# One step for both head groups: the products with k and v of batches 2 to 7 in a fused attention and expert kernel

## The chip, the cores and the metric

The kernel runs on one core of a Trainium2 chip. A core has TensorE (PE in the profile, with its weight loads as PEld), VectorE (DVE), ScalarE (ACT), GpSimd (POOL) and SyncE (SP); in this kernel SP does nothing but issue DMAs, and POOL issues some as well. The metric is device time in microseconds (us). One execution was profiled; the others were only timed.

## The reference

For 8 batches and 8 heads, with sequence 576, head width 64 and 32 memory slots, the attention is

```python
a = softmax(phi, over the sequence)          # (b, h, 576, 32)
k_m = einsum('bhsm,bhsd->bhmd', a, k)        # 32 x 64 per head
v_m = einsum('bhsm,bhsd->bhmd', a, v)
attn = softmax(q @ k_m.T / 8)                # (b, h, 576, 32)
x = attn @ v_m                               # 4608 rows of 512
```

and its result feeds four dense experts, weighted per row: `out += p[:, e] * (relu(x @ w1[e]) @ w2[e])`, with 512 inputs, 1024 hidden and 512 outputs. The change concerns the two einsums: the contraction over the 576 sequence places that gives k_m and v_m.

## The kernel before, in words

The kernel never forms x. It multiplies v_m with w1 (helper `vw_mm`, L433) and applies the attention weights to that product (`first`, L548 to L550; six matmuls in a step, three for each of two weight halves because operands are split into a high and a low part). `second` (L581 to L583) multiplies the hidden values with w2.

**Steps.** The first part of the program, up to about 400 us, is a list of 128 steps. Each step `s` emits, in this order: `accumulate()`, then `run_plan(s)`, then `first(s + 2)` and `second(s)`. Every engine runs its own instructions in the order in which they were emitted. `run_plan(s)` emits whatever the table `plan` holds for step `s`: the attention of the next batches, the splits of w2, stores and loads. The rest of the program, from step 128, works by another scheme and is not touched.

**Attention of batch b** (`attention`, L649 onward) hangs on a number `turn` from the table `ATT`: 30, 46, 62, 77, 92 and 107 for batches 2 to 7. At `turn` and after, exp(phi) is transposed; at `turn + 6` the products for the first four heads (group 0) run, at `turn + 9` those of the other four (group 1); each is read out of its accumulator by ScalarE one step later (`kv_out`, L304); at `turn + 11` both are transposed (`kv_fold`, L312), and at `turn + 12` copied (`kv_pick`).

**One group's product** is two calls of `kv_mm` (`c2` = 0 and 1), each with eight matmuls of a 32-column weight (L292) that read one staged tile of k and v, 128 x 1024 numbers or 512 KB; the second call adds four matmuls with the tail of the sequence (L298). A batch so needs four staged tiles, two for each group.

**Staged tiles.** All tiles that are streamed in (k and v, q, the raw w2) pass through one sequence, `order`, in the order in which the steps take them, and through four buffers of 512 KB. Taking tile i (`take`) emits the load of tile i + 3 on SP's queue. SP runs its queue strictly in order and does not keep to the steps: a load starts when all issues ahead of it have gone out and its buffer has been read by everyone who reads it. Which of the four buffers a load gets is fixed when the program is built, and with it whom it waits for. A w2 tile is read in two steps, by ScalarE (L153) and then by POOL (L154), once for each half.

In the same 128 steps SP's queue carries w1 (L158), phi (L238), the tail (L242), w2 once more for sums of its columns (`sv`, L191), the exchange of v_m (`vs`, L475), outputs (L606) and, near the end, w2 halves written earlier (`w<-kw`, L752).

Of the kernel before, what the change touches and what calls it, by code (L numbers as in the profile page):

```python
# [51 lines left out]
    7: (99, 107, (2 * PAIR + 112, 2 * PAIR + 116, 2 * PAIR + 123), (2 * PAIR + 120, 2 * PAIR + 125, 2 * PAIR + 131)),  # L52
}

SCORES_0 = ((2, 0), (4, 1))
SCORES_1 = ((0, 8), (2, 9), (4, 13))
VW_1 = (11, 15)
# [24 lines left out]
def body(ctx: ExitStack, tc: tile.TileContext, qm, qt, kv, kvt, phi, prob, w1, w1d, w2, out):  # L82
# [8 lines left out]
    def bank(tag, *shape):  # L91
        n = idle[tag].popleft()
        out = banks[:, n, :]
        m = 1
        for d in shape:
            m *= d
        names = "abcd"[:len(shape)]
        out = out[:, :m].rearrange(
            f"p ({' '.join(names)}) -> p {' '.join(names)}", **dict(zip(names, shape))
        )  # L100
        lent[id(out)] = tag, n, out
        return out

    def give(ps):
        tag, n, _ = lent.pop(id(ps))
        idle[tag].append(n)
# [128 lines left out]
    def load_phi(b):  # L235
        ph = att.tile([P, 2, S], F32, name="ph", tag="ph")
        for g in range(2):
            nc.sync.dma_start(ph[:, g], phi[b, g])  # L238
        st["ph", b] = ph

    def load_tail(b):
        nc.sync.dma_start(kvt_t[64:], kvt[b])  # L242

    def phi_max(b, g):
        nm = att.tile([P, 1], F32, name="nm", tag="nm", bufs=2)
        nc.vector.reduce_max(nm, st["ph", b][:, g], AX.X)
        nc.vector.tensor_scalar_mul(nm, nm, -1.0)
        st["nm", b, g] = nm

    def phi_exp(b, g):  # L250
        ph = st["ph", b][:, g]
        zs = att.tile([P, 1], F32, name="zs", tag="zs", bufs=4)
        nc.scalar.activation(ph, ph, AF.Exp, bias=st["nm", b, g], accum_out=zs)
        st["zs", b, g] = zs

    def phi_norm(b, g):
        zs = st["zs", b, g]
        nc.vector.tensor_scalar_add(zs, zs, 1e-9)
        nc.vector.reciprocal(zs, zs)

    def phi_turn(b, g):
        if g == 0:
            st["a", b] = att.tile([P, 2, NC, P], F32, name="a", tag="a")
        ph = st["ph", b]
        tp = bank("pm", 4, P)
        for c in range(4):
            nc.tensor.transpose(tp[:, c], ph[:, g, c * P:c * P + P], ident)
        st["tpa", b, g] = tp

    def phi_turn_out(b, g, copy=nc.scalar.copy):  # L270
        copy(st["a", b][:, g, :4], st["tpa", b, g])
        give(st["tpa", b, g])

    def phi_turn_tail(b):

        tp = bank("pm", 2, P)
        for g in range(2):
            nc.tensor.transpose(tp[:, g], st["ph", b][:, g, S - P:], ident)
        st["tpb", b] = tp

    def phi_turn_tail_out(b, copy=nc.scalar.copy):
        copy(st["a", b][:, :, 4], st["tpb", b])
        give(st["tpb", b])

    def kv_mm(b, g, c2, raw):
        if c2 == 0:
            st["x", b, g] = bank("pm", P)
        x, a = st["x", b, g], st["a", b]
        for i in range(2):
            for h in range(4):  # L290
                m = slice(M * h, M * h + M)
                nc.tensor.matmul(  # L292
                    x[m], a[:, g, 2 * c2 + i, m], raw[:, i, h], start=c2 + i == 0, stop=False,
                    skip_group_check=True,
                )
        for h in range(4 if c2 else 0):
            m = slice(M * h, M * h + M)
            nc.tensor.matmul(  # L298
                x[m], a[:, g, 4, m], kvt_t[:, 4 * g + h], start=False, stop=True, skip_group_check=True
            )  # L300

    def kv_out(b, g):
        xs = att.tile([P, 2 * P], F32, name="xs", tag="xs", bufs=3)[:, :P]
        nc.scalar.activation(xs, st["x", b, g], AF.Copy, scale=st["zs", b, g])  # L304
        give(st["x", b, g])
        st["xs", b, g] = xs

    def kv_fold(b, gs=range(2)):
        for g in gs:
            if g == gs[0]:  # L310
                st["kvp", b, g] = bank("pm", len(gs), P)
            nc.tensor.transpose(st["kvp", b, gs[0]][:, g - gs[0]], st["xs", b, g], ident)  # L312

    def kv_pick(b, gs=range(2), copy=nc.scalar.copy):
        src = st["kvp", b, gs[0]]
        n = 2 * len(gs)
        copy(
            kvm[b % 6][:, 2 * gs[0]:2 * gs[0] + n].rearrange("p a j m -> p (a j m)"),
            src.rearrange("p g m -> p (g m)"),
        )  # L320
        give(src)
# [14 lines left out]
    def scores_mm(b, t0, q, hps=range(NP)):  # L336

        nt, n = tiles(t0)
        if hps[0] == 0:
            st["sT", b, t0] = [bank("pm", 256) for _ in range(2)]  # L340
        sT = st["sT", b, t0]
        for hp in hps:
            for i in range(2):
                half, m = slice(64 * i, 64 * i + 64), slice(M * hp, M * hp + M)
                nc.tensor.matmul(
                    sT[i][m, :nt * n], kvm[b % 6][half, hp, i], q[half, hp, :nt * n],
                    start=True, stop=True,
                )
# [49 lines left out]
    def q_key(b, t0):  # L398
        return ("qm", b, t0 // 2) if t0 < 4 else ("qt", b)
# [60 lines left out]
    def v_split(b):  # L460

        vh = att.tile([P, 2, NP, M], F32R, name="vh", tag="xs", bufs=3)
        for j in range(2):
            r = v_half(j)
            split(vh[r], kvm[b % 6][r, :, j], nc.gpsimd)
        st["vh", b] = vh

    def write_v(b):

        if b == 4:  # L470
            st["vs"] = att.tile([P, 2, NP, P], F32R, name="vs", tag="vs")
        c = slice(M * (b - 4), M * (b - 4) + M)
        for j in range(2):
            for i in range(2):
                nc.sync.dma_start(  # L475
                    st["vs"][64 * i:64 * i + 64, j, :, c].bitcast(F32),
                    st["vh", b][v_half(j), i].bitcast(F32),
                )
# [139 lines left out]
    def at(s, unit):  # L618
        plan[s].append(unit if isinstance(unit, tuple) else (None, unit))

    def scores_quick(b, t0, n):

        at(n, (q_key(b, t0), lambda q: (scores_mm(b, t0, q), scores_copy(b, t0))))
        at(n + 1, lambda: (scores_turn(b, t0), scores_max(b, t0)))
        at(n + 2, lambda: (scores_exp(b, t0), soft_sum(b, t0)))
        at(n + 3, lambda: soft_scale(b, t0, nc.vector))
        at(n + 4, lambda: (transposes(b, t0), transposes_out(b, t0)))
# [5 lines left out]

    for t0, n in SCORES_0:
        scores_quick(0, t0, n)
# [19 lines left out]
    def attention(b, s, turn, scores, turns):  # L655

        at(s, lambda: load_phi(b))
        at(turn, lambda: load_tail(b))
        for g in range(2):
            at(s + 3, lambda g=g: phi_max(b, g))  # L660
            at(s + 4, lambda g=g: phi_exp(b, g))
            at(s + 5, lambda g=g: phi_norm(b, g))
            at(turn + g, lambda g=g: phi_turn(b, g))
            at(turn + 1 + g, lambda g=g: phi_turn_out(b, g))
        at(turn + 2, lambda: phi_turn_tail(b))
        at(turn + 3, lambda: phi_turn_tail_out(b))
        for g in range(2):
            for c2 in range(2):
                at(turn + 6 + 3 * g, (("kv", b, g, c2), lambda raw, g=g, c2=c2: kv_mm(b, g, c2, raw)))
            at(turn + 7 + 3 * g, lambda g=g: kv_out(b, g))  # L670
        at(turn + 11, lambda: kv_fold(b))
        at(turn + 12, lambda: kv_pick(b))
        if b >= 4:
            at(turn + 15, lambda: v_split(b))
            at(turn + 17, lambda: write_v(b))
        for t0, n in zip((0, 2, 4), scores):
            at(n, (q_key(b, t0), lambda q, t0=t0: scores_mm(b, t0, q)))
            plan[n + 1].insert(0, (None, lambda t0=t0: scores_copy(b, t0)))
            at(n + 2, lambda t0=t0: scores_turn(b, t0))
            at(n + 3, lambda t0=t0: scores_max(b, t0))  # L680
            at(n + 4, lambda t0=t0: scores_exp(b, t0))
            at(n + 5, lambda t0=t0: soft_sum(b, t0))
            at(n + 6, lambda t0=t0: soft_scale(b, t0, nc.gpsimd))
        for t0, n in zip((0, 2, 4), turns):
            at(n, lambda t0=t0: transposes(b, t0))
            at(n + 1, lambda t0=t0: transposes_out(b, t0))
# [27 lines left out]
    for b in range(2, B):  # L714
        attention(b, *ATT[b])
# [288 lines left out]
    with tc.manual_schedule():  # L1004
        raw = {}
# [9 lines left out]
        raw = {key: take(later) for later, key in enumerate(early)}  # L1015
# [128 lines left out]
```

## Time and profile before

| | us |
|---|---|
| median of 3 timed runs | 1333.23 (1332.06 to 1333.5) |
| profiled execution, own time | 1333.66 |
| its span | 1331.9 |
| PE busy | 1313.2 (99%) |
| DVE busy | 813.6 (61%) |
| POOL busy | 587.2 (44%) |
| ACT busy | 535.8 (40%) |

The clock granted to TensorE is shown as a share of full speed; over the span its mean was 0.999. "Idle before" in a row of the timeline is time in which the engine had nothing running, followed by what ended it. A DMA row with "q" behind the engine is the issue of a transfer, not the transfer; its time to landing is told in the view of the DMAs. Line numbers are those of the kernel before; in the changed kernel the lines behind the new table are one higher.

### The profile page before, as it was taken

The numbers are of one execution on the slowest core, as the hardware profiler recorded it, in microseconds if no ns is written. First come the engines' busy times: TensorE is split into PE (matmuls) and PEld (weight loads), VectorE is DVE, ScalarE is ACT, GpSimd is POOL, SyncE is SP. The second block draws the span as 40 slices with busy tenths as digits, with TensorE's granted clock in tenths as the row PEclk, the third lists the DMA queues.
The fourth block names the chain that finished last, engine by engine and source line by source line (L and its number), as shares of the span: only waits on it lengthen the run. The fifth ranks groups of instructions, "written<-read, shape, count | busy, mean of one in ns | idle before, by whom it ended". The sixth has DMA issues, their size and how long they took to land.

```text
span 1331.9 us, 27463 instructions
## 1 busy us (share of the span) xinstructions
PE 1313.2 (99%) x10232; PEld 1192.4 (90%) x10232; DVE 813.6 (61%) x1882; ACT 535.8 (40%) x1303; POOL 587.2 (44%) x666
## 2 busy tenths in 40 slices
PE   8999999999999999999999999999999999999998
PEld 6777878877889888889999999999999999999998
DVE  3544545444336676767666766767677766666665
ACT  3424435435223443333445445554434333333332
POOL 1104336314104553333576677776744433433342
PEclk9999999999999999999999999999999999999999
DMA  8445966956634663234479999999976865656551
GB/s 295 136 180 185 340 221 217 356 185 231 218 131 186 254 252 118 94 143 159 174 261 347 339 342 321 313 330 321 305 218 190 250 189 169 178 163 187 165 171 72
DMA packets 93014, 296.53 MB, mean 223 GB/s; under 512 B 16977, under 2 KB 18129, under 8 KB 92881
## 3 DMA queue, kind: packets, MB, share of 16 engines
q1 hardware_dynamic: 74448, 227.66, 52.5%
q0 software_dynamic: 17280, 62.92, 12.1%
q10 hardware_dynamic: 1152, 4.19, 0.8%
q8 instruction: 81, 1.33, 0.4%
q14 instruction: 53, 0.43, 0.1%
HBM read 217.65 MB, written 76.55 MB: 221 GB/s over the span
## 4 chain that ended last, share of the span: by engine, by line
PE 88%; DMA 4%; DVE 4%; issue 2%; POOL 1%; ACT 1%; SPq 0%; DVEq 0%; POOLq 0%; ACTq 0%
PE banks L891 35%; PE banks L805 7%; PE banks L807 7%; PE banks L806 7%; PE banks L582 4%; PE banks L581 4%; PE banks L583 4%; PE banks L548 2%; PE banks L494 2%; PE banks L433 2%; DMA v<-sv 2%; PE banks L550 2%; PE banks L549 2%; PE banks L929 2%; PE banks L930 2%; PE banks L931 2%
## 5 line engine op out<-in xcount | busy, mean ns | idle before, releaser
L909 DVE SCALAR_TENSOR_TENSOR acc<-banks,pt,acc 128x256 f32<-128x256 f32 x624 | 298.7, 480 | 172.6 <-PE banks L891 168.4
L891 PE MATMUL banks<-w,half 128*128 128x256 f32 x2016 | 300.5, 282 | 1.9 <-DVE acc L909 1.9
L891 PEld LDWEIGHTS banks<-w,half 128*128 128x128 f32 x2016 | 272.4, 189 | 13.4 <-DVE acc L909 4.2
L807 PE MATMUL banks<-AT,vw 128*128 128x256 f32 (+1 forms) x768 | 227.7, 296 | 0.0
L806 PE MATMUL banks<-AT,vw 128*128 128x256 f32 (+1 forms) x768 | 227.4, 296 | 0.0
L805 PE MATMUL banks<-AT,vw 128*128 128x256 f32 (+1 forms) x768 | 227.2, 296 | 0.0
L872 POOL TENSOR_TENSOR half<-g,half 128x512 fp32r<-128x512 f32 x96 | 124.6, 1298 | 158.3 <-ACT half L871 112.6
L154 POOL TENSOR_TENSOR w<-stage,w 128x512 fp32r<-128x512 f32 x96 | 126.0, 1316 | 110.5 <-ACT w L153 108.3
L882 POOL TENSOR_TENSOR n<-xs,n 128x256 fp32r<-128x256 f32 x96 | 70.9, 739 | 174.6 <-ACT n L881 88.1
L805 PEld LDWEIGHTS banks<-AT,vw 128*128 128x128 f32 x768 | 145.4, 189 | 0.9 <-DVE hm L820 0.2
L806 PEld LDWEIGHTS banks<-AT,vw 128*128 128x128 f32 x768 | 144.8, 189 | 0.1
L807 PEld LDWEIGHTS banks<-AT,vw 128*128 128x128 f32 x768 | 144.5, 188 | 0.0
L857 ACT ACTIVATE half<-banks 128x512 fp32r<-128x512 f32 x96 | 57.4, 598 | 207.1 <-DVE g L863 165.2
L562 DVE SCALAR_TENSOR_TENSOR h<-banks,h 128x256 fp32r<-128x256 f32 x128 | 53.8, 421 | 119.0 <-ACT h L560 78.2
L207 POOL TENSOR_TENSOR sv<-sv 128x512 fp32r<-128x512 f32 x32 | 41.2, 1291 | 138.1 <-DVE sv L201 94.9
L582 PE MATMUL banks<-w,h 128*128 128x512 f32 x256 | 100.9, 394 | 0.0
L581 PE MATMUL banks<-w,h 128*128 128x512 f32 x256 | 100.7, 393 | 0.0
L583 PE MATMUL banks<-w,h 128*128 128x512 f32 x256 | 100.7, 393 | 0.0
L560 ACT ACTIVATE h<-banks 128x256 fp32r<-128x256 f32 x128 | 49.0, 384 | 110.5 <-PE banks L550 105.7
L881 ACT CAST n<-xs 128x256 fp32r<-128x256 f32 x96 | 38.6, 402 | 134.2 <-DVE xs L879 134.2
L863 DVE SCALAR_TENSOR_TENSOR g<-banks,g 128x256 f32<-128x256 f32 x192 | 72.3, 418 | 26.6 <-PE banks L807 23.6
L819 ACT ACTIVATE hm<-banks 128x128 fp32r<-128x128 f32 x96 | 26.7, 278 | 152.3 <-DVE xs L879 119.4
(133 smaller groups left out, 2718.4 us busy)
## 6 DMA issues: line engine op xcount, KB each, us to landing
w<-kw SPq DMA_DIRECT2D x91, 512.0 KB, 5.8
w<-v SPq DMA_DIRECT2D x82, 512.0 KB, 5.4
vwd<-vst POOLq DMA_DIRECT2D x64, 512.0 KB, 6.4
vw<-vwd SPq DMA_DIRECT2D x256, 128.0 KB, 5.8
stage<-in_kv SPq DMA_DIRECT2D x32, 512.0 KB, 6.0
w<-in_w SPq DMA_DIRECT2D x32, 512.0 KB, 7.1
v<-sv POOLq DMA_DIRECT2D x32, 512.0 KB, 6.2
stage<-in_w1d SPq DMA_DIRECT2D x32, 512.0 KB, 5.8
```

Source lines behind the costliest of these rows:

```text
L154: eng.tensor_sub(dst[:, 1, :], raw, dst[:, 0, :].bitcast(F32))
L581: nc.tensor.matmul(po[t], x[:, 0, :], w[:, 0, :], start=j == 0, stop=False)
L582: nc.tensor.matmul(po[t], x[:, 0, :], w[:, 1, :], start=False, stop=False)
L583: nc.tensor.matmul(po[t], x[:, 1, :], w[:, 0, :], start=False, stop=j == NJ - 1)
L805: nc.tensor.matmul(ps, w[:, 0, f], at_t[:, g, 0, c], start=g == 0, stop=False)
L806: nc.tensor.matmul(ps, w[:, 0, f], at_t[:, g, 1, c], start=False, stop=False)
L807: nc.tensor.matmul(ps, w[:, 1, f], at_t[:, g, 0, c], start=False, stop=g == 1)
L863: VE.scalar_tensor_tensor(d[:, i], src, 0.0, g[:, 1 + i], ALU.max, ALU.subtract)
L872: GP.tensor_sub(D[:, 1], d, D[:, 0].bitcast(F32))
L882: GP.tensor_sub(N4[:, 1], n, N4[:, 0].bitcast(F32))
L891: nc.tensor.matmul(ps, a[:, l, jj], w[:, r, c], start=start and jj + i == 0, stop=jj == 1 and i == 2, skip_group_check=True,)
L909: VE.scalar_tensor_tensor(a, src, p, a, ALU.mult, ALU.add)
```

## The change

A new table, `KV_AT`, names for each of batches 2 to 7 one step at which all four products of the batch are emitted, group 0 and then group 1; both results are read out in the step behind it.

```diff
+KV_AT = {2: 36, 3: 52, 4: 68, 5: 86, 6: 101, 7: 113}
 ...
         for g in range(2):
             for c2 in range(2):
-                at(turn + 6 + 3 * g, (("kv", b, g, c2), lambda raw, g=g, c2=c2: kv_mm(b, g, c2, raw)))
-            at(turn + 7 + 3 * g, lambda g=g: kv_out(b, g))
+                at(KV_AT[b], (("kv", b, g, c2), lambda raw, g=g, c2=c2: kv_mm(b, g, c2, raw)))
+            at(KV_AT[b] + 1, lambda g=g: kv_out(b, g))
         at(turn + 11, lambda: kv_fold(b))
         at(turn + 12, lambda: kv_pick(b))
```

For batches 2, 3, 4 and 7 the step is `turn + 6`: group 1 moves three steps forward. For batches 5 and 6 it is `turn + 9`: group 0 moves three steps back. No instruction is added or removed. Steps of the products, before and now:

| batch | group 0 before | group 1 before | both now |
|---|---|---|---|
| 2 | 36 | 39 | 36 |
| 3 | 52 | 55 | 52 |
| 4 | 68 | 71 | 68 |
| 5 | 83 | 86 | 86 |
| 6 | 98 | 101 | 101 |
| 7 | 113 | 116 | 113 |

On PE, batch 2 before, around steps 36 and 39. `stage_1271`, `stage_1324`, `stage_1371` and `stage_1400` are the batch's four staged tiles in their order; the matmuls that read AT are `first`.

```order
L583 MATMUL banks_72<-w2_1303,h_1336 128x512
L292 MATMUL banks_72<-stage_1271,a_1248 32x128 x8
L292 MATMUL banks_72<-stage_1324,a_1248 32x128 x8
L298 MATMUL banks_72<-tail_84,a_1248 32x128 x4
L548 MATMUL banks_72<-AT_279,vw_1092 128x256
```

```order
L583 MATMUL banks_72<-w2_1373,h_1432 128x512
L292 MATMUL banks_72<-stage_1371,a_1248 32x128 x8
L292 MATMUL banks_72<-stage_1400,a_1248 32x128 x8
L298 MATMUL banks_72<-tail_84,a_1248 32x128 x4
L548 MATMUL banks_72<-AT_279,vw_1006 128x320
```

The same place in the changed kernel:

```order
L584 MATMUL banks_72<-w2_1303,h_1336 128x512
L293 MATMUL banks_72<-stage_1271,a_1248 32x128 x8
L293 MATMUL banks_72<-stage_1324,a_1248 32x128 x8
L299 MATMUL banks_72<-tail_84,a_1248 32x128 x4
L293 MATMUL banks_72<-stage_1371,a_1248 32x128 x8
L293 MATMUL banks_72<-stage_1400,a_1248 32x128 x8
L299 MATMUL banks_72<-tail_84,a_1248 32x128 x4
L549 MATMUL banks_72<-AT_279,vw_1092 128x256
```

The third and fourth tile are now read directly behind the first two, with nothing of `first` or `second` between.

On SP's queue, batch 6 before. The batch's four tiles are `stage_3155`, `stage_3214`, `stage_3299` and `stage_3309`; `stage_3266` is the last raw w2 tile, `stage_3399` and `stage_3409` are the first two of batch 7.

```order
L139 DMA stage_3155<-in_kv 128x1024
L139 DMA stage_3214<-in_kv 128x1024
L139 DMA stage_3266<-in_w2 128x1024
L158 DMA w1_3277<-in_w1 128x1024
L139 DMA stage_3299<-in_kv 128x1024
L139 DMA stage_3309<-in_kv 128x1024
L139 DMA stage_3338<-in_qt 128x256
L238 DMA ph_3353<-in_phi 128x576 x2
L158 DMA w1_3380<-in_w1 128x1024
L139 DMA stage_3399<-in_kv 128x1024
```

And now:

```order
L140 DMA stage_3155<-in_w2 128x1024
L140 DMA stage_3214<-in_kv 128x1024
L140 DMA stage_3266<-in_kv 128x1024
L159 DMA w1_3277<-in_w1 128x1024
L140 DMA stage_3314<-in_kv 128x1024
L239 DMA ph_3327<-in_phi 128x576 x2
L159 DMA w1_3354<-in_w1 128x1024
L140 DMA stage_3373<-in_kv 128x1024
L140 DMA stage_3383<-in_qt 128x256
L140 DMA stage_3397<-in_kv 128x1024
```

The raw w2 tile (now `stage_3155`) comes ahead of the batch's four (now `stage_3214`, `stage_3266`, `stage_3314`, `stage_3373`), and the fourth stands behind phi and a pair of w1 loads (here one row of the two). As the program is built, `stage_3373` goes into the buffer of that w2 tile and waits for POOL's second reading of it.

## The prediction

> **What bounds the kernel now.** I read the page first, then the waits, then the timeline at the products with k and v.
>
> ```profile
> span 1331.9 us, 27463 instructions
> PE 1313.2 (99%) x10232; PEld 1192.4 (90%) x10232; DVE 813.6 (61%) x1882; ACT 535.8 (40%) x1303; POOL 587.2 (44%) x666
> stage<-in_kv SPq DMA_DIRECT2D x32, 512.0 KB, 6.0
> ```
>
> TensorE sets the time: it is idle for 18.7 us of the whole span, so nothing that another engine does faster can bring much, and every wait put on PE lengthens the end. The third row is the one to keep in mind: a staged tile of k and v takes a median of 6.0 us from issue to landing, and a batch needs four.
>
> ```profile
> PE banks L292 <- DMA stage<-in_kv: 2.5, 4, 0.9
> SPq L139 <- POOL w L154: 180.3, 32, 31.8
> SPq L139 <- PE banks L292: 69.9, 11, 19.7
> ```
>
> These are rows of the waits (total us, times, longest). PE hardly waits for those tiles today. SP, though, waits long with the staged loads, for POOL's splits of w2 and for PE's own reading: the loads go out when a buffer comes free, so some go out late. The question is how late the fourth tile of each batch is against the step that now wants all four.
>
> **The work itself.** The timeline of PE, batch 2 (start, us, and the idle time in brackets if there is any):
>
> ```profile
> 135.61 0.40 PE L583 MATMUL banks<-w,h 128*128 128x512 f32 x1
> 135.94 1.08 PE L292 MATMUL banks<-stage,a 128*32 128x128 f32 x32
> 136.84 0.40 PE L298 MATMUL banks<-tail,a 128*32 128x128 f32 x8
> 137.17 0.39 PE L548 MATMUL banks<-AT,vw 128*128 128x256 f32 x1
> 137.39 0.28 PE L549 MATMUL banks<-AT,vw 128*128 128x256 f32 x1
> 137.51 0.28 PE L550 MATMUL banks<-AT,vw 128*128 128x256 f32 x1
> 143.81 1.08 PE L292 MATMUL banks<-stage,a 128*32 128x128 f32 x32
> ```
>
> One group takes 137.17 - 135.94 = 1.23 us: two tiles at 0.45 each (to 136.84) and the tail at 0.33. All of it stays; only its place moves. What the merging saves is the change of shapes: the first matmul behind a group takes 0.22 to the next (137.17 to 137.39) where the second takes 0.12, so 0.10, and I put the entry at as much again. Six visits fewer at 0.20 make **-1.2 us**. If the hardware hides that, it is 0.
>
> ScalarE reads out two results in one step instead of one in each of two; it is busy 40% of the span and the transposes behind it stay at `turn + 11`, so I cost that at nothing. For one step two accumulator banks of four are held, at steps 52 and 113 beside a third for transposes, so that the next `first` reuses the bank of the one just before it. Covered by the `second` between them; if not, I allow up to 0.5 us at each.
>
> **The waits, batch by batch.** Now the step wants the third tile 1.23 us after its start and the fourth 1.23 + 0.45 = 1.68 us after it.
>
> Batch 2, all at step 36 (135.94). The fourth tile goes out when POOL has split the last w2 half:
>
> ```profile
> 135.69 1.70 POOL L154 TENSOR_TENSOR w<-stage,w 128x512 fp32r<-128x512 f32 x1 [0.80 <-ACT w L153]
> 137.41 0.33 SPq L139 DMA_DIRECT2D stage<-in_kv  x1
> stage<-in_kv SPq DMA_DIRECT2D x1, 512.0 KB, 3.6
> ```
>
> It lands at 137.41 + 3.6 = 141.0. Before, PE came for it after 143.81 and found it there. Now PE comes at 135.94 + 1.68 = 137.6: a wait of **3.4 us**. Nothing ahead of that load in POOL's or SP's queue is moved.
>
> Batch 4, step 68:
>
> ```profile
> 227.48 0.33 SPq L139 DMA_DIRECT2D stage<-in_kv  x1
> stage<-in_kv SPq DMA_DIRECT2D x1, 512.0 KB, 6.9
> 228.32 0.68 SPq L139 DMA_DIRECT2D stage<-in_kv  x1
> stage<-in_kv SPq DMA_DIRECT2D x1, 512.0 KB, 8.6
> 227.61 1.08 PE L292 MATMUL banks<-stage,a 128*32 128x128 f32 x32
> 236.97 0.65 PE L292 MATMUL banks<-stage,a 128*32 128x128 f32 x16 [0.40 <-DMA stage<-in_kv]
> ```
>
> The third tile lands at 234.4, the fourth at 236.9. The fourth goes out just as PE has read the first, whose buffer it is given in the changed program as well, so it cannot be early for a step that reads both. PE wants the third at 227.61 + 1.23 = 228.8: 5.5 us; reads it until 234.85; and waits 2.1 for the fourth. 7.6, less the 0.40 that it waited anyway: **7.2 us**. In the new order a q load stands behind these two and holds phi and the `sv` loads back until PE has read the third tile; if that thins the traffic so that both land in the median 6.0, the fourth lands at 234.3 and the sum is 4.6.
>
> Batch 6, step 101. The raw w2 tile of step 99 now precedes the batch's four in the sequence, and the fourth tile takes its buffer, which POOL frees with its second half. Before, the first tile of batch 7 stood at that point:
>
> ```profile
> 322.09 1.30 POOL L154 TENSOR_TENSOR w<-stage,w 128x512 fp32r<-128x512 f32 x1 [1.31 <-DMA stage<-in_kv]
> 323.41 0.33 SPq L139 DMA_DIRECT2D stage<-in_kv  x1
> stage<-in_kv SPq DMA_DIRECT2D x1, 512.0 KB, 6.3
> 324.44 1.08 PE L292 MATMUL banks<-stage,a 128*32 128x128 f32 x32
> ```
>
> With group 0 gone from step 98, steps 99 to 101 come 1.23 us earlier, and ScalarE and POOL with them: issue at 322.2, landing at 328.5. PE reaches the fourth at 324.44 - 1.23 + 1.68 = 324.9: **3.6 us**. If POOL is not earlier the landing is 329.7 and the wait 4.8; two loads fewer ahead of it in the queue could bring it down to 3.
>
> Batch 7, step 113. Here the fourth load stands behind outputs that VectorE has to finish:
>
> ```profile
> 354.30 1.38 SPq L606 DMA_DIRECT2D out<-acc  x2
> 356.45 0.49 SPq L139 DMA_DIRECT2D stage<-in_kv  x1
> stage<-in_kv SPq DMA_DIRECT2D x1, 512.0 KB, 5.1
> 357.21 1.08 PE L292 MATMUL banks<-stage,a 128*32 128x128 f32 x32
> ```
>
> Landing 361.55, wanted at 358.9: **2.7 us**. The queue up to that load is as before.
>
> Batches 3 and 5 I cost at nothing:
>
> ```profile
> 161.67 1.35 SPq L139 DMA_DIRECT2D stage<-in_kv  x1
> 182.08 1.08 PE L292 MATMUL banks<-stage,a 128*32 128x128 f32 x32
> 266.23 1.39 POOL L212 DMA_DIRECT2D v<-sv  x2
> 282.52 1.08 PE L292 MATMUL banks<-stage,a 128*32 128x128 f32 x32
> ```
>
> The fourth tile of batch 3 goes out 20 us ahead of its step. That of batch 5 now stands behind the `sv` and phi loads, which wait for stores that POOL issues by 267.6; with some 6 us for those, 1.5 for four issues and 6.0 for the tile it lands by about 281, wanted at 282.52 - 1.23 + 1.68 = 283.0. Cover 2 us; a store 3 us later would cost 1.
>
> Sum of the waits: 3.4 + 7.2 + 3.6 + 2.7 = 16.9, less 1.2 for the merging: **+15.7 us**. Behind a waiting product stand `first` and `second` of the same step, whose operands are ready; they cannot fill the hole, since PE runs in order. After it the other engines follow PE's pace, so I see nothing that gives the time back.
>
> **The clock.** Waits of this size have a second price, seen in the one halving of this trace (columns: PE, PEld, DVE, ACT, POOL, granted clock, DMA share and rate):
>
> ```profile
> 24.75:28.17 3.42, 2.12 (x24) 1.04 (x23) 2.76 (x6) 1.75 (x5) 0.06 (x1) 1.00 1.05 294
> 28.17:31.58 3.41, 3.41 (x12) 2.72 (x12) 0.43 (x1) 1.29 (x4) 1.29 (x1) 0.50 0.68 183
> 28.29 0.42 PE L548 MATMUL banks<-AT,vw 128*128 128x256 f32 x1
> 28.50 0.42 PE L549 MATMUL banks<-AT,vw 128*128 128x256 f32 x1
> ```
>
> A stretch of 3.41 us in which PE was idle for 1.30 is followed by one at half clock, where a 256-column matmul takes 0.21 to the next instead of 0.12: 3.41 x (1 - 0.12/0.21) = 1.5 us lost. Each of the four waits, 2.7 us or more, leaves at least 1.35 idle in one of the two stretches that it can fall into. A halved stretch that begins inside the wait costs only its rest, and now and then two are halved; I take 1.3 a wait, **+5.2 us**. Bounds: 0 if one such event is chance, 8 x 1.5 = 12 if two stretches follow each wait.
>
> The Trainium skill speaks against my row here: the page TensorE: Matmul & The Clock Gate, under "HAM oscillation — how this bites in real kernels", sums the rule up as "no PE-idle gaps >~3.4µs". The trace does not bear that out as a safe limit: the idle 1.30 us above was enough. What it would make of the time stands among the rivals.
>
> **Sum.** Against the profiled execution: 1333.66 + 15.7 + 5.2 = 1354.6. That execution is 0.4 above the median of the runs, so 1354 us.
>
> **Rivals.**
> *The waits come, the clock holds.* For it: there is one halving only, and other short waits passed without. If only a stretch that is idle throughout is halved, then of the four only batch 4's 5.5 us can hold one, and not surely: 1333.2 + 15.7 + 0 to 1.5, some 1349 to 1350. That is the Trainium skill's rule at work. Against: the rows just shown.
> *The waits come larger.* Loads of batch 4 share the engines with POOL's stores, and a delayed PE may meet another pattern; with the upper ends (batch 6 at 4.8, both banks 0.5, two halved stretches a wait) 1333.2 + 15.7 + 1.2 + 1 + 12 = 1363.
> *The loads are there in time, and the merging pays.* SP runs ahead of the steps; for batches 3 and 5 the fourth tile lands before its step. Were it so for all, there would remain -1.2 and the 0.4 of batch 4: 1331.6. It decides at an issue 4 to 7 us before the step's fourth product; in batches 2, 4, 6 and 7 the issue lies between 0.7 us after PE's step began and 2.7 us before PE's want, with the buffer freed no sooner. So it needs another buffer assignment than the one built.
> *It does nothing that can be measured* (0.2% is 2.7 us, what a measurement of this kernel can tell): only two of the waits would have to be there, and small.
>
> **Chances.** Forecast 0.54; clock holds 0.30; larger 0.10; in time and faster 0.03; nothing 0.03. So slower 0.94, same 0.03, faster 0.03. The range is from 1345 (batch 4 at 4.6, batch 6 at 3, clock held: 1333.2 + 13.7 - 1.2 = 1345.7) to 1361, leaving out the far part of the larger case.
>
> **What would show it.** In the changed profile: PE waiting at L293 for `stage<-in_kv` four times by 2 to 6 us, near steps 36, 68 (twice), 101 and 113, about 17 us in all; none at 52 and 86; the fourth loads issued at the same point against PE as here; half clock in a stretch behind each wait; from step 128 on the same length as before. No such wait, or the buffer of a fourth tile free 6 us before its step, would make the prediction wrong; waits of that size at full clock would make the last term wrong.

## The result, and the profile after

The changed kernel takes **1354.18 us** (median of 5 runs, 1353.2 to 1356.28); the kernel before, run beside it, takes 1333.5 (1332.06 to 1334.64). The ratio is **1.0157, with a 95% interval of 1.0146 to 1.0168**: 20.7 us slower, against a forecast of 1354 us. The profiled execution has a span of 1352.3 us, 20.4 more than before.

The head of its page:

```profile
span 1352.3 us, 27463 instructions
PE 1317.3 (97%) x10232; PEld 1197.2 (89%) x10232; DVE 813.4 (60%) x1882; ACT 536.1 (40%) x1303; POOL 587.2 (43%) x666
```

The instruction counts are the same and DVE, ACT and POOL do the same work. PE is idle for 35.0 us where it was idle for 18.7, and it is busy for 4.1 us longer with the same matmuls. So 16.3 us went into waits, and 4.1 us into the same matmuls running slower, net of what merging saves.

The view of the waits (total us, times, longest), and PE's timeline at the products (start, us, idle time in brackets):

```profile
PE banks L293 <- DMA stage<-in_kv: 17.5, 9, 5.1
PE banks L346 <- ACT kvm L318: 1.3, 1, 1.3
```

```profile
138.55 0.64 PE L293 MATMUL banks<-stage,a 128*32 128x128 f32 x16 [1.15 <-DMA stage<-in_kv]
141.24 0.64 PE L293 MATMUL banks<-stage,a 128*32 128x128 f32 x16 [2.04 <-DMA stage<-in_kv]
186.40 1.08 PE L293 MATMUL banks<-stage,a 128*32 128x128 f32 x32
187.51 1.06 PE L293 MATMUL banks<-stage,a 128*32 128x128 f32 x32
237.94 1.08 PE L293 MATMUL banks<-stage,a 128*32 128x128 f32 x16 [5.05 <-DMA stage<-in_kv]
240.56 1.08 PE L293 MATMUL banks<-stage,a 128*32 128x128 f32 x16 [1.53 <-DMA stage<-in_kv]
294.67 1.06 PE L293 MATMUL banks<-stage,a 128*32 128x128 f32 x32
339.72 0.65 PE L293 MATMUL banks<-stage,a 128*32 128x128 f32 x16 [3.00 <-DMA stage<-in_kv]
378.23 0.77 PE L293 MATMUL banks<-stage,a 128*32 128x128 f32 x16 [2.88 <-DMA stage<-in_kv]
```

Batches 2, 4, 6 and 7 wait (rows 1 and 2, 5 and 6, 8, 9); batch 3 (rows 3 and 4) and batch 5 (row 7, its second group) run straight through. Before, line L292 waited 2.5 us for staged tiles in the whole program.

The windows view, in stretches of 3.41 us that begin where the granted clock can change (PE, PEld, DVE, ACT and POOL busy, granted clock, DMA):

```profile
136.26:139.67 3.41, 1.79 (x56) 1.28 (x49) 1.81 (x2) 0.00 (x0) 1.29 (x1) 1.00 0.31 93
139.67:143.09 3.42, 1.85 (x32) 1.61 (x33) 0.00 (x0) 0.05 (x1) 0.00 (x0) 1.00 0.99 400
231.83:235.25 3.42, 1.06 (x40) 0.79 (x32) 0.42 (x1) 1.79 (x4) 2.97 (x4) 1.00 1.02 314
235.25:238.66 3.41, 0.72 (x16) 0.65 (x16) 0.00 (x0) 0.13 (x1) 3.39 (x5) 0.50 0.98 360
238.66:242.07 3.41, 1.88 (x33) 1.07 (x25) 0.00 (x0) 0.00 (x0) 1.72 (x3) 0.50 1.03 416
242.07:245.49 3.42, 3.42 (x11) 3.03 (x12) 0.43 (x1) 0.90 (x3) 0.55 (x1) 0.50 1.03 417
337.65:341.06 3.41, 1.34 (x28) 1.14 (x29) 0.00 (x0) 0.00 (x0) 0.00 (x0) 1.00 0.96 369
341.06:344.48 3.42, 3.42 (x12) 2.85 (x11) 2.05 (x5) 0.90 (x3) 0.00 (x0) 0.50 0.02 8
375.19:378.61 3.42, 0.54 (x24) 0.38 (x20) 0.00 (x0) 0.00 (x0) 0.00 (x0) 1.00 0.95 344
378.61:382.02 3.41, 3.41 (x29) 2.83 (x18) 0.12 (x1) 0.66 (x3) 0.00 (x0) 0.50 0.51 199
```

The wait of batch 4 is followed by three stretches at half clock, those of batches 6 and 7 by one each, that of batch 2 by none. A matmul of 512 columns behind 341.06 comes every 0.43 us, not every 0.23.

Where the time went, step by step: the start of `first` in each step of the changed kernel, less its start in the kernel before, and by how much that difference moves. (Where a group of products leaves a step, the step gets shorter, so a pair of plus and minus belongs together.)

| batch | steps | moves, us | sum |
|---|---|---|---|
| 2 | 36, 39, 42 | +4.69, -1.32, +0.89 | +4.26 |
| 3 | 52, 55 | +1.09, -1.32 | -0.23 |
| 4 | 68, 69, 71 | +9.18, +1.58, -1.92 | +8.84 |
| 5 | 83, 86 | -1.32, +1.09 | -0.23 |
| 6 | 98, 101, 102 | -1.33, +4.29, +1.38 | +4.34 |
| 7 | 113, 114, 116 | +4.51, +1.22, -1.32 | +4.41 |

The sum is 21.4. What moves elsewhere (the first 50 us, where a halved stretch falls differently, and small moves later) takes back 0.7 of it in all: the last `first` of this part starts 20.7 us later than before. From there to the end the two kernels run in step to within 0.4 us.

### The profile page after: what moved, and what is told of

It reads as the page before. It is cut to its first block, busy times and chain, and to the rows that moved or that the text cites. A ratio compares the mean times of both kernels' runs of the same rounds, so it can differ in the third digit from the quotient of the medians.

```text
span 1352.3 us, 27463 instructions
## 1 busy us (share of the span) xinstructions
PE 1317.3 (97%) x10232; PEld 1197.2 (89%) x10232; DVE 813.4 (60%) x1882; ACT 536.1 (40%) x1303; POOL 587.2 (43%) x666
## 3 DMA queue, kind: packets, MB, share of 16 engines
q8 instruction: 81, 1.33, 0.4%
## 4 chain that ended last, share of the span: by engine, by line
PE 88%; DMA 5%; DVE 3%; POOL 1%; issue 1%; ACT 1%; SPq 0%; POOLq 0%; ACTq 0%; DVEq 0%
PE banks L892 35%; PE banks L806 7%; PE banks L808 7%; PE banks L807 7%; PE banks L582 4%; PE banks L583 4%; PE banks L584 4%; DMA stage<-in_kv 3%; PE banks L549 3%; PE banks L495 2%; PE banks L551 2%; PE banks L550 2%; PE banks L434 2%; PE banks L930 2%; PE banks L931 2%; PE banks L932 2%
```

## Experiments

The first theory is that of the prediction: four late loads, the halved clock behind them, and a small saving at each merging. The main rival: merging itself costs, for instance by reading two results out at once, holding more accumulator banks or shifting the order on ScalarE and SP; then each of the six batches would carry some 3.5 us, and the waits would be a symptom.

### Merging the two batches whose tiles are early

Only batches 3 and 5 keep their row of the table; the others are emitted as before. Against the changed kernel:

```diff
-KV_AT = {2: 36, 3: 52, 4: 68, 5: 86, 6: 101, 7: 113}
+KV_AT = {3: 52, 5: 86}
 ...
+            n = KV_AT.get(b, turn + 6 + 3 * g)
 ...
-            at(KV_AT[b] + 1, lambda g=g: kv_out(b, g))
+            at(n + 1, lambda g=g: kv_out(b, g))
```

> Only batches 3 and 5 in one step, the other four as before. If the price is the wait for late loads, these two cost nothing and save the change of shapes twice: 0.2 to 0.25 us each, so 1333.0, no wait for staged tiles at steps 52 and 86. If merging itself costs (two results read out at once, three banks held), a third of the 20.7 us should stay: about 1340.

Measured: 1332.71 us, ratio to before 0.9996 (0.9986 to 1.0006). The kernel before was run beside the experiments: it took 1333.27 us beside this one and the next three, 1332.56 us beside the last four, and the differences given below are to these. The second group of each, in PE's timeline:

```profile
183.16 1.06 PE L293 MATMUL banks<-stage,a 128*32 128x128 f32 x32
282.51 1.06 PE L293 MATMUL banks<-stage,a 128*32 128x128 f32 x32
```

No wait stands in either row. Between the two kernels' timelines both batches gain 0.23 us (+1.09 where a group joins, -1.32 where it leaves), as in the table above; the whole is too small for the timed runs. In these two batches merging has no price of its own, and the rival, which would have left a third of the 20.7 us, falls.

### Filling the waits with matmuls

All six merged; ahead of a product that has to wait, PE multiplies the identity by itself into a free bank.

```diff
+WARM = {(2, 1, 0): 4, (2, 1, 1): 7, (4, 1, 0): 18, (4, 1, 1): 5, (6, 1, 1): 11, (7, 1, 1): 10}
 ...
     def kv_mm(b, g, c2, raw):
 ...
+        if (b, g, c2) in WARM:
+            keep_warm(WARM[b, g, c2])
```

> All six merged, and PE runs matmuls of the identity on itself into a free bank while it waits in batches 2, 4, 6 and 7, as many as fit at 0.26 us each (4 and 7; 18 and 5; 11; 10). The products still come when their tiles land. If the halved clock costs time of its own, no stretch of half clock is left there and 5 to 5.5 us go: about 1349. If the half clock is only a mark of the waits, 1354. If the extra matmuls outlast the waits, up to 1355.

Measured: 1347.81 us (1.0109, 1.0096 to 1.0122), 14.5 us over the kernel before in place of 20.7: 6.1 are gone. Batch 2 in PE's timeline, and the stretches of batches 4, 6 and 7 in the windows view:

```profile
136.93 1.83 PE L1004 MATMUL banks<-ident 128*128 128x128 f32 x14
138.69 0.64 PE L296 MATMUL banks<-stage,a 128*32 128x128 f32 x16
```

```profile
228.60:242.30 13.70, 11.53 (x147) 9.90 (x146) 0.85 (x2) 2.83 (x7) 9.26 (x12) 1.00 0.99 375
332.00:345.00 13.00, 13.00 (x130) 11.18 (x123) 4.96 (x16) 4.23 (x16) 0.00 (x0) 1.00 0.43 163
370.00:378.00 8.00, 7.04 (x64) 6.15 (x63) 1.17 (x3) 2.00 (x7) 0.00 (x0) 1.00 0.55 218
```

The clock stays whole in all four places, and each product begins within 0.1 us of the landing of its tile, except in batch 6, where the extra matmuls outlast the tile by 0.4 us (it lands at 334.71, and the product begins at 335.10). By the starts of `first`, as in the table above, the sums of batches 4, 6 and 7 fall from 8.84, 4.34 and 4.41 us to 7.28, 2.55 and 3.37, together by 4.4 us; that of batch 2, behind which nothing had been halved, stays (4.26, now 4.34). The rest of the difference between the two profiles lies in their first 50 us, ahead of these products: the changed kernel's profile has one halved stretch near 27 us that this execution does not have and that comes and goes (in five of the ten profiles of this study something like it stands within the first 32 us). So the half clock is a cost of its own, and it can be had back without making a tile land earlier. What is left is the waits, less what merging saves.

### The fourth load of batch 7 queued earlier

```diff
+        if b == 7:
+            at(106, lambda: stage_ahead(60))
```

> All six merged; the fourth load of batch 7 is put on SP's queue at step 106 rather than at 113, ahead of the outputs of step 112; its buffer is free since step 104. Waits theory: the 2.9 us at step 113 and the half clock behind it (1.5) go, nothing else changes: about 1349.8. If batch 7's price lies elsewhere, 1354.

Measured: 1349.38 us (1.0122, 1.0109 to 1.0135), 16.1 us over the kernel before in place of 20.7: 4.6 are gone, as forecast. SP's queue and PE's second group at step 113:

```profile
350.64 0.87 SPq L140 DMA_DIRECT2D stage<-in_kv  x2
374.59 1.06 PE L293 MATMUL banks<-stage,a 128*32 128x128 f32 x32
```

The load goes out over 20 us ahead instead of behind the outputs of step 112, and neither a wait nor a halved stretch is left there. By the starts of `first`, the sum of batch 7 falls from +4.41 us to -0.23. (In this execution batches 2 and 6 lost 1.3 and 0.9 us more than in the changed kernel's profile, and the first 50 us about 2 us less.) What held this tile was its place in SP's queue.

### Buffers of their own for group 1

The two tiles of group 1 get memory that the first part of the program does not use, and the rule that emits loads counts only the four shared buffers.

```diff
+            if apart(i):                       # kv of group 1, batches 2 to 7
+                t = att.tile([P, 1024], F32, name="stage", tag="Y", bufs=2)
-            if STAGE <= i < STAGE + 4:
+            elif STAGE <= i < STAGE + 4:
 ...
-        stage_ahead(i + STAGE if i >= len(early) else i + 1)
+        upto, ring = i, 0
+        while upto < len(order) and (apart(upto) or ring < STAGE):
+            ring += not apart(upto)
+            upto += 1
+        stage_ahead(upto if i >= len(early) else i + 1)
```

> All six merged, with the two tiles of group 1 of each batch loaded into two buffers of their own (in memory that the first part does not use), so that no w2 split and no reading of the same step holds them. If the late loads are the whole price: no waits at steps 68, 101 and 113, up to 1.2 us at step 36 (those loads still stand behind the second tile's), full clock, 1332 to 1335. If merging or its order on the other engines costs, 1350 or more.

Measured: 1345.11 us (1.0092, 1.0079 to 1.0105). Of the 20.7 us only 8.9 are gone: a miss. The waits at steps 101 and 113 are gone, as expected; one of 1.29 us is left at step 68, where none was expected; and a new one stands at step 74. In the timelines of PE, DVE and SP:

```profile
257.38 0.46 PE L356 MATMUL banks<-stage,kvm 64*32 64x64 f32 x14 [6.13 <-DVE hm L573]
254.06 0.75 DVE L257 TENSOR_REDUCE nm<-ph 128x1 f32<-128x576 f32 x1 [6.67 <-DMA ph<-in_phi]
239.95 1.32 SPq L146 DMA_DIRECT2D stage<-in_kv  x3
241.32 0.96 SPq L249 DMA_DIRECT2D ph<-in_phi  x2
```

Three loads for batch 5 that nobody needs before step 86 now go out ahead of the phi of the same batch, which step 72 needs. The first half of phi lands 12.7 us after its issue; DVE, in order, stands before the maximum of phi; the hidden values behind it are late; and PE stands. Here the loads put earlier were paid by the one that they were put ahead of. Batch 2, forecast to wait up to 1.2 us, kept waits of 0.72, 2.00 and 0.40 us, although its second, third and fourth tile were issued within 0.9 us (at 129.83, 130.26 and 130.74): they landed 6.2, 8.6 and 9.2 us later. So these tiles are held by the transfers that are under way with them, not only by buffers.

### Own buffers in batches 4, 6 and 7 only

```diff
-        return kind == "kv" and b >= 2 and g[0] == 1
+        return kind == "kv" and b in (4, 6, 7) and g[0] == 1
```

> All six merged; own buffers for group 1's two tiles in batches 4, 6 and 7 only, so that the loads of batch 5 no longer pass the phi load of step 69. If that passing made the 6 us stop at step 74 of the run with own buffers for all: it is gone, a wait of 1.3 us stays at step 68, none at 101 and 113, and batch 2 keeps its 3.2 us, the 0.9 more at step 42 and 0 to 2.5 of half clock: 1336 to 1340. If the stop comes from the merging in batch 4, it stays: 1343 or more.

Measured: 1339.65 us (1.005, 1.0036 to 1.0065), inside the forecast. PE at steps 36, 68 and 74:

```profile
138.68 0.65 PE L303 MATMUL banks<-stage,a 128*32 128x128 f32 x16 [2.20 <-DMA stage<-in_kv]
232.08 0.65 PE L303 MATMUL banks<-stage,a 128*32 128x128 f32 x16 [1.15 <-DMA stage<-in_kv]
249.42 0.34 PE L356 MATMUL banks<-stage,kvm 64*32 64x64 f32 x14 [1.17 <-DVE hm L573]
```

With batch 5's own buffers gone, two of its loads rather than four go out ahead of phi, and the stop at step 74 falls from 6.13 to 1.17 us, with a second one of 1.04 behind it. So most of it came from the passed load, not from the merging in batch 4. What is left fits the same cause: DVE still waits 1.59 and 1.01 us for the two halves of phi. The 0.9 us at step 42, which the forecast had kept, did not come; why is told below.

### The same with batch 2 three steps later

`KV_AT` has 39 in place of 36 for batch 2.

> The same with batch 2 at step 39 (group 0 moved back) in place of 36. The fourth tile then has three more steps, 8 us, to land: batch 2 costs nothing, 1332 to 1335. If batch 2's price is not the lateness of its tiles, as the run before.

Measured: 1334.29 us (1.0014, 1.0005 to 1.0023): 5.4 us less than the run before by moving one batch to a step at which its tiles are nearly there. One wait of 0.51 us is left at step 39 of the profiled execution, the slowest of the ten (1338.63 us). Batch 2's price was lateness as well. Some 1.7 us over the kernel before remain, with the waits at steps 68 and 74 still there.

### Batch 4 alone

`KV_AT` holds only batch 4, at 68.

> Batch 4 alone merged, at step 68. Ledger of the changed kernel: two waits of 6.2 us more than before together and a half clock of 2 to 3 us, less 0.2: 8.8 us, so 1342. If the prices of the batches feed each other, well off that.

Measured: 1341.28 us (1.0069, 1.0053 to 1.0085), 8.7 more than before beside it.

```profile
232.74 1.08 PE L293 MATMUL banks<-stage,a 128*32 128x128 f32 x16 [4.80 <-DMA stage<-in_kv]
236.05 1.08 PE L293 MATMUL banks<-stage,a 128*32 128x128 f32 x16 [2.23 <-DMA stage<-in_kv]
```

Two waits of 7.03 us in all (6.58 with the other batches merged too). The 8.84 us that the table above gives to this batch come out by themselves, so its price does not hang on the other batches.

### Merging only where the tiles are in time

No buffers added; batch 2 at 39, 3 at 52, 5 at 86, 7 at 113 with its load queued at step 106; 4 and 6 as before.

> No buffers added. Merged only where the four tiles land before the step: batch 2 at 39, 3 at 52, 5 at 86, 7 at 113 with its fourth load queued at step 106; batches 4 and 6 as before. Waits theory: four times 0.23 us saved, nothing lost: 1332.5 (1332 to 1334), at or under the kernel before. If merging has a price of its own: 1338 or more.

Measured: 1331.87 us, ratio 0.9995 (0.9985 to 1.0005). Step 39 has the only wait in the four merged steps:

```profile
143.52 0.64 PE L293 MATMUL banks<-stage,a 128*32 128x128 f32 x16 [0.17 <-DMA stage<-in_kv]
```

Batches 3, 5 and 7 gain 0.23 us each between the timelines, and batch 2 loses 0.14 at steps 36 and 39, so 0.55 us in all are gained. That is in the trace; the timed runs cannot tell this kernel from the one before. It is the best use of the idea that was found, and it does not beat the kernel before by anything that can be measured.

## Why the prediction was right

**The waits.** Forecast 16.9 us in four batches, measured 15.3 more than before: batch 2 3.19 (forecast 3.4), batch 4 6.58 less 0.40 (7.2), batch 6 3.00 (3.6), batch 7 2.88 (2.7). The landing of the fourth tiles repeated what the trace of before showed for the load at the same point of the queue: 3.6, 8.2, 5.8 and 5.2 us from issue to landing, against 3.6, 8.6, 6.3 and 5.1. Two details were off. In batch 2 part of the wait came for the third tile, which I had left out:

```profile
131.75 0.33 SPq L140 DMA_DIRECT2D stage<-in_kv  x1
stage<-in_kv SPq DMA_DIRECT2D x1, 512.0 KB, 6.7
```

It landed at 138.4. In this execution the step began at 136.10, so the fourth's wait would have begun at 136.10 + 1.68 = 137.8; the third came 0.6 us behind that, and the one wait became two with the same end. And holding phi and `sv` back at step 68 did not thin the traffic: third and fourth tile took 6.3 and 8.2 us, near the 6.9 and 8.6 of before, not the median.

**The mergings.** Forecast 1.2 us saved for six, measured 0.23 each in batches 3 and 5; if the other four save as much, 1.4.

**The clock.** Forecast 5.2 us, and some 5.5 by PE's busy time (4.1 longer, and the 1.4 that merging should have saved), but the working was not right in its parts. A halved stretch costs 3.41 x (1 - 0.23/0.43) = 1.6 us if PE is busy throughout. Batch 6 and 7 had one whole one each, 3.2; behind batch 4 the half clock lasted 10.2 us, of which PE had work in some 6 (from 237.94 to 245.49 less the 1.53 of waiting), 2.8 us by the same share. Counted so it is 6.0 in all, which agrees with the busy time within the roughness of both. Against that, batch 2's waits halved nothing, although PE was idle for 1.6 us in both stretches, more than the 1.30 on which I built the rule. The step that failed is "leaves at least 1.35 idle in one of the two stretches": that row of before was not a threshold. What the runs show in its place is told below. That 1.3 a wait came out near the mean is partly luck: none behind batch 2, some 2.8 behind batch 4.

The rival by the Trainium skill's rule (TensorE: Matmul & The Clock Gate, "HAM oscillation — how this bites in real kernels"), under which gaps of up to some 3.4 us do no harm, is not borne out: the waits of 3.00 and 2.88 us in batches 6 and 7 were followed by one halved stretch each.

**Costed at nothing.** Batches 3 and 5: right. Reading two results in one step: right at steps 53 and 114, no wait. I had not forecast the 0.9 us more at step 42:

```profile
157.04 0.67 PE L346 MATMUL banks<-stage,kvm 64*32 64x256 f32 x16 [1.28 <-ACT kvm L318]
155.71 0.62 ACT L207 CAST sv<-sv 128x512 fp32r<-128x512 f32 x1 [3.23 <-DMA v<-sv]
156.61 0.37 ACT L318 COPY kvm<-banks 128x256 f32<-128x256 f32 x1
```

The copy that PE waits for stands in ScalarE's queue behind a cast, and the cast waits for the landing of a store issued by POOL. That store is issued 4.9 us later than before (at 147.83, before at 142.97), as late as step 36 had become, and lands 4.2 us later (155.56, before 151.32). PE, which had got the 1.3 us of step 39 back by then, comes only 3.5 us later. It hangs on how long the store takes: 7.7 us here, but 5.4 in the run with batch 7's load queued earlier and 6.6 in that with own buffers in batches 4, 6 and 7, and in these two no wait stands at step 42. In the changed kernel it is the one place where a delay made another wait longer; elsewhere the delays neither grew nor were won back, as forecast.

The three runs with own buffers add one thing: with batch 4 merged and its tiles nearly in time, step 69 is 0.8 to 1.0 us longer than before. Its `first` comes directly behind transposes and waits 0.65 us (in the run with own buffers in batches 4, 6 and 7) until VectorE has read the result of an earlier `first`. That is what the prediction feared at steps 52 and 113 from banks held by two products, at up to 0.5 us; that the held banks cause it was not shown.

**The total.** That 15.7 + 5.2 = 20.9 came so close to 20.7 is partly luck too: the waits were put 1.6 us too high, and 0.9 us at step 42 were not forecast.

**What stays open.** The cause of step 69's delay, and the first 50 us, which differ from execution to execution by more than the merging saves. Not tried: a fifth shared buffer.

## What to carry to other kernels

Work that reads streamed tiles can be packed into one step for next to nothing, but only as many tiles as have landed by then; before moving it, read off for each tile who frees its buffer, what stands ahead of it in the issuing queue, and add the landing time from the trace. A load moved forward can hold up those that it passes: batch 7's cost nothing, batch 5's cost a stop of 6.1 us, because an engine that runs in order handed the delay on to work that never touched them. Here waits of TensorE of some 3 us cost about half as much again through the clock in batches 6 and 7, and nothing in batch 2; dummy matmuls in the hole bought that part back where the tile itself came no sooner.

## What the runs showed of the hardware

The granted clock of TensorE changed only on a fixed grid of 3.41 us: in the changed kernel's profile the changes at 235.25, 245.49, 341.06, 344.48, 378.61 and 382.02 lie 3, 31, 32, 42 and 43 such stretches behind the first. Over ten profiles of this kernel and its variants, after step 30 of the program a stretch at full clock in which PE was idle for 1.89 us or more was always followed by one at half clock (1.89, 1.91, 2.04, 2.07, 2.20, 2.36, 2.88 and four that were wholly idle; the stretch in which the program ends is left aside), and one with 1.80 or less never was (1.80, 1.63, 1.57, 1.56, 1.43). Within a halved stretch less idle time is enough to keep it: 1.53 us in the rows above, and 0.77 in the run with batch 7's load queued earlier; 0.40 in the run with own buffers for all batches was not. In the first 30 us, where PE runs many small matmuls, stretches with 1.30 and 1.44 us idle were halved and others with 1.55 were not, so it is not idle time alone that counts there; what else does was not tried. Whether a given wait is halved thus depends on where it falls on the grid: batch 2's 3.2 us were split into 1.63 and 1.56 in one execution, and in the run with batch 7's load earlier waits of 2.9 us in all at the same place were followed by two halved stretches.
